# Attention and FFN in one kernel: weight loads after the first U transpose, a 64-row FFN tile of two chunks computed as a pair, and new planner constants

## The chip, the cores and the metric

One core of a Trainium2 chip. The metric is the device time of one execution in microseconds; the profile's span runs from the first to the last profiled instruction of that core.

## The reference

S = 2048 tokens, D = 640, H = 32 query heads of 20 columns, one shared key and value head, FFN width F = 1728, all in bfloat16.

```
xn = layernorm(x)
q = (xn @ wq) in 32 heads of 20;  k = xn @ wk;  v = xn @ wv      # one k and v for all heads
p = softmax(q k^T / sqrt(20));    o = p v                        # per head, 2048 x 2048
h = silu(xn @ w1)                                                # 1728 columns
return x + concat(o) @ wo + h @ w2
```

## The kernel before, in words

**Order.** The kernel holds its own planner. Every operation is an `Op` with an engine, a planned duration and dependencies; `Sched` lets engines and planned times run, picks for each engine the next operation that is ready, and writes down one fixed order per engine. The waits are semaphores between these orders. So a changed constant or a changed operation can move instructions anywhere on any engine. SP issues nearly all DMAs, in its order.

**Attention.** The queries are cut into four chunks of 512 (`QC = 4`). A unit is one head of one chunk, 128 in all; three units make a group, and the 43rd group has two. A group has 16 steps, one for each block of 128 keys (688 steps in all). In a step:

- `do_S` issues the score matmuls, one for each unit, in tiles of 32 rows of the PE array side by side (L773), into three PSUM banks; steps use two sets of banks in turn.
- ACT takes the exponential of two or three of the units in one instruction (L791, 1024 or 1536 columns).
- In most steps `want_dve` gives the third unit to DVE instead, which forms the exponential from integer bits: L805 clips the scores into `Z`, L873 adds a constant for up to three such blocks at a time, and POOL adds another one (L811). The three versions are added up with different weights in the PV matmuls.
- `pv_mm` issues the value matmuls (L861), four tiles of 32 columns side by side, into one bank (`UBANK`). Those that use POOL's sum (the "thirds") are put together by `flush_z`.

`want_dve` refuses steps named in `KT_ACT`, the first eight steps, and steps at which the work planned for DVE exceeds `DVE_TH`.

**End of a group.** `end_group` copies the bank to `U` on DVE (L976). `norm_dma` transposes `U` into `UT` by a DMA from SP (L935), POOL reads the result (L946, L943, L948), DVE takes reciprocals (L953) and POOL writes the normalized heads into `o` (L962). For the very last group PE does the transpose (L988).

**Jobs between the steps.** `step` fills PE's time between score matmuls with PV passes or with the next matmul of a job, taken in order from one queue: query projections (`qd_job`, L1054, evicted on DVE and spread to `qT` by some seven DMAs from SP, L1070), FFN first layer (`h_job`, L1090; tanh on ACT, L1098, and a product on DVE, L1103, since silu is made from tanh), and output jobs (`out_job`, FFN second layer L1152, attention output L1157). `fill_chunk` lists the jobs of a chunk and their earliest steps; `H_FIRST` FFN jobs come before the output jobs of the chunk before. `fill` adds matmuls on zeros where PE would be idle (L697, L710). When few slots of the exponentials' ring are left (`PV_PRESS`), PV goes first.

F = 1728 makes 13 tiles of 128 rows and one of 64 (`FLAST`); each of the four chunks computes all 14 (`fk` 0 to 13), five matmuls each. The second layer uses the 64-row tile with `w2[0:64, 13]`.

**Late loads.** `late_loads` issues from SP what is needed later: 14 pieces of `w2` (L1336), five of `wo` (L1519), and a fill of the second half of `qT` from `tb` (L1512, 1 MB). POOL then scales `wo` in place (L1522, five times). It is called with a key on which the loads depend: in `qd_job`, at the first query job of chunk 0. `tb[0]` is also where the tanh of even FFN tiles goes.

**End of the kernel.** Behind the last step stand the last output jobs: first `hold_job` (L1215, L1220), which opens banks with the residual and the attention output of four blocks, then the last block of heads, transposed on PE (L1130, evicted at L1135), and the closing matmuls (L1157), ACT and DVE evictions (L1184, L1187) and output DMAs (L1191).

Of the kernel before, what the change touches and what calls it, by code (L numbers as in the profile page):

```python
# [14 lines left out]
P = 128  # L15
# [3 lines left out]
DC = 5  # L19
SLOT = 32  # L20
BANK = 512
QW = 512
# [5 lines left out]
FC = 14  # L28
FLAST = F - 13 * P
# [16 lines left out]
NBLK = 31  # L46
NZ = 4
ZB = 3
AHEAD = 30
Q_FROM = 8  # L50
H0_STEP = 10
KT_ACT = ()
Y_POOL = True
Y_TIME = 0.72
Y_LOCK = False
Y_SLOW = 0.1
H_FIRST = 8
NEARLY = 2
LASTPV = 16
DVE_LAST = 1  # L60
ZWAIT = 6
SWITCH = 0.105
S_LEAD = 0.56
PV_PRESS = 8
DVE_TH = 2.6
U_PRIO = 1.1
X_PRIO = 0.8
PACE = (0.9, 0.9, 0.9, 0.9)
# [273 lines left out]


class Job:
    def __init__(self, name, mms, reads, consume, gate=None, min_step=-1, banks=None, on_start=None, width=0, hold=None, use=None):
# [10 lines left out]
        self.use = use  # L356


class Builder:
# [371 lines left out]
    def do_mm(self, job, now, d):  # L731
        work, fn = job.mms.pop(0)
        job.begun = True
        b = job.bank
        op = self.sc.new("pe", d, lambda pe: fn(pe, b), job.reads, [("B", b)], name=job.name, queue=False)
        op.work = min(work, 0.009) if job.name[0] == "v" else min(work, 0.053) if job.name[0] == "t" else work
# [17 lines left out]
    def do_S(self, t, now):  # L754
        sc = self.sc
        g, kt = divmod(t, KT)
# [10 lines left out]
        def fn(pe):  # L767
            ins = None
            for j, x in enumerate(us):
# [7 lines left out]
        op = sc.new("pe", 0.216 + self.switch("S"), fn, self.s_reads(t, dv), [("B", par3 + j) for j in range(nh)],  # L777
                    name=f"S{t}", queue=False)
# [36 lines left out]
        first = kt == 0  # L815
        last = kt == KT - 1

        if dv:
            y = self.Y[:, zs, 0, zp * QW:(zp + 1) * QW].bitcast(BF16)
            z = self.Z[:, zs, zp * QW:(zp + 1) * QW].bitcast(BF16)  # L820
        thirds = []

        def pfn(pe):
# [9 lines left out]
            for x in thirds:  # L833
# [3 lines left out]
                    name=f"PV{t}", mode="PV", queue=False)  # L837
# [10 lines left out]
        if self.zblocks and (len(self.zblocks) >= (ZB if g < self.NG - 2 else 2) or t - self.zblocks[0][0] >= ZWAIT  # L848
                             or t == self.T - 1 or (kt == KT - 1 and g >= FLUSH_G)):
            self.flush_z()  # L850
        self.move_pv()
        if last:
            self.end_group(g)
# [10 lines left out]
    def flush_z(self):  # L864
        sc = self.sc
        zs = self.zset
        n = len(self.zblocks)
        self.zset = (self.zset + 1) % NZ
        zk = [("Z", zs, i) for i in range(n)]
        Z = self.Z[:, zs, 0:n * QW]  # L870
        w = n * QW
        for k in range(1 if self.y_on_pool else 2):
            sc.new("dve", Y_SLOW + t_dve_4x(w), lambda v, k=k: v.tensor_scalar(  # L873
                self.Y[:, zs, k, 0:n * QW], Z, float(PH[k + 1][0]), None, ALU.add), zk,
                [("Y", zs, k, i) for i in range(n)], prio=4.0 + 0.1 * k, name=f"y{k}").lock = True
        ts = []
        for i, (t, pv) in enumerate(self.zblocks):
            ks = [("Z", zs, i), ("Y", zs, 0, i)]
            pv.deps |= sc.deps_of(ks, ())
            for k in ks:  # L880
                sc.readers[k].append(pv)
            x = self.Y[:, zs, 1, i * QW:(i + 1) * QW].bitcast(BF16)
            kt = t % KT

            def th(pe, q, x=x, kt=kt):
                if q >= 2:
                    return self.pv_mm(pe, q, 2, kt, x, False, False)
# [3 lines left out]
        first = self.zblocks[0][1]  # L891
        end = self.pv_wait[-1][0].kt == KT - 1
        tail = self.pv_wait.pop() if end else None
        seen = False
        for op, _ in self.pv_wait:
            seen = seen or op is first
            if seen and self.can_host(op) and ts:
                self.host(op, ts.pop())
        if end and self.can_host(tail[0]) and len(self.thirds + ts) % 3 == 1:
            self.host(tail[0], ts.pop() if ts else self.thirds.pop())  # L900
        self.thirds += ts
        while len(self.thirds) >= 3 or (end and self.thirds):
            part = self.thirds[:3]
# [12 lines left out]
            self.pv_wait.append((op, False))  # L916
        if tail is not None:
            self.pv_wait.append(tail)
        self.zblocks = []

    def can_host(self, op):
        return op.after is not None and not op.after and op.kt < KT
# [8 lines left out]
    def norm_dma(self, g, rows):  # L931
        sc = self.sc
# [4 lines left out]
        op.dur = UT_ISSUE  # L937
        self.ut_cnt[up] += 1
        op.inc_no = self.ut_cnt[up]
        ut = self.UT[:, up, :, :].rearrange("p q (i j) -> p q i j", j=SLOT)  # L940
        w = self.W
        if rows == P:
# [104 lines left out]
    def qd_job(self, c, m, step=-1):  # L1047
# [10 lines left out]
        def consume(b):  # L1058
            sl = self.nqd % 2
            self.nqd += 1  # L1060
            sc.new("dve", t_dve_ps(QW), lambda v: v.tensor_scalar(self.qd[0:rows, sl, :], self.bk(b, 0, QW, 0, rows), C1,
                                                                  None, ALU.mult), [("B", b)], [("qd", sl)],
                   prio=X_PRIO, name=f"qev{c}_{m}")
            sem = sc.sem(f"q{c}_{m}")
            ops = []
            heads = range(lo // DH, -(-hi // DH))
            for h in heads:
                a, z = max(lo, h * DH), min(hi, h * DH + DH)
                r = (h % 4) * SLOT + a - h * DH
                ops.append(sc.dma("sp", lambda q, a=a, z=z, r=r, h=h: q.dma_start(  # L1070
                    self.qT[r:r + z - a, h // 4, c % 2, :], self.qd[a - lo:z - lo, sl, :]), [("qd", sl)],
                    [("qb", c % 2, h)], (z - a) * QW * 2, sem=sem, name="qdma"))
                ops[-1].dur = 0.74
            sc.note(ops[-1], (), [("q", c, h, lo) for h in heads])
            for op in ops:
                op.inc_no = len(ops)
            if c == 0 and m == 0:
                self.late_loads(("qd", sl))
        reads = [("xnT", 4 * c + i) for i in range(4)] + [("wqd", 0), ("wqd", 1)]
        if c >= 2:  # L1080
            step = max(step, self.first_step[c - 1] + KT)
# [1 line left out]

    def h_job(self, c, fk, step):
        sc = self.sc
        rows = P if fk < FC - 1 else FLAST
        mms = []
        for k in range(DC):
            def f(pe, b, k=k):
                return pe.matmul(self.bk(b, 0, QW, 0, rows), self.w1[:, k, fk * P:fk * P + rows],  # L1090
                                 self.xnT[:, k, c * QW:(c + 1) * QW], start=(k == 0), stop=(k == DC - 1))
            mms.append((t_mm(QW), f))

        def consume(b):
# [6 lines left out]
            if c == 0:  # L1101
# [4 lines left out]
        reads = [("xnT", 4 * c + i) for i in range(4)] + [("w1",)]  # L1106
        return Job(f"h{c}_{fk}", mms, reads, consume, min_step=step, width=QW if rows == P else 0)

    def try_oT(self, c):
        last = c == QC - 1  # L1110
# [29 lines left out]
    def out_job(self, c, i, e, step=-1, ffn=True, ks=range(DC), src="xres", dst="ost", hmax=H):  # L1140
# [5 lines left out]
        tot = (FC if ffn else 0) + len(ks)  # L1146
        if ffn:
            for fk in range(FC):
                rows = P if fk < FC - 1 else FLAST

                def f(pe, b, fk=fk, rows=rows, m=len(mms)):
                    return pe.matmul(self.bk(b, 0, 320), self.hT[0:rows, fk, i * P:(i + 1) * P],  # L1152
                                     self.w2[0:rows, fk, e0:e0 + 320], start=(m == 0), stop=(m == tot - 1))
                mms.append((t_mm(320), f))
        for k in ks:
            def f(pe, b, k=k, m=len(mms)):
# [76 lines left out]
    def fill_chunk(self, c, t):  # L1233
# [58 lines left out]
    def prologue(self):  # L1292
# [370 lines left out]
```

## Time and profile before

| what | us |
|---|---|
| median of 6 runs | 738.34 |
| lowest, highest run | 736.34, 739.56 |
| the profiled execution, time | 736.35 |
| the profiled execution, span | 734.6 |
| first score matmul of the last group (L773) | 706.45 |
| last score matmul (L773) | 719.16 |
| U copied for the first transpose, DVE L976 | 50.50 to 51.19 |
| first U transpose, SP L935: issued, landed | 55.10, 61.13 |
| qT fill behind the late loads, SP L1512: issued, landed | 54.36, 60.56 |

Group rows read: line, engine, operation, out<-in with shapes, count, then busy time and the mean of one in ns, then idle time of the engine just before and what ended it. Window rows read: stretch, then busy time and count on PE, PE's weight loads, DVE, ACT and POOL, then granted PE clock, share of the DMA engines, GB/s. Wait rows: who waited for whom, total, times, longest. Timeline rows: start, length, engine, line, with the idle time before in brackets. Busy time is the union of instructions that can overlap: consecutive ones on an engine can start less than a duration apart.

### The profile page before, as it was taken

How to read it: one execution, taken by the hardware profiler on the slowest of the kernel's cores; microseconds unless marked ns; L12 is line 12 of the kernel's file. 1: busy time of each engine (PE TensorE's matmuls, PEld its weight loads, DVE VectorE, ACT ScalarE, POOL GpSimd, SP SyncE). 2: the span in 40 equal slices, each digit the busy share in tenths (PEclk: the TensorE clock that was granted, in tenths of full speed). 3: DMA queues.
4: the chain of work that ended last, by engine and by line, in shares of the span. 5: the costliest groups of instructions: out<-in, count | busy, mean ns of one | idle time of the engine just before them, and what ended most of it. 6: DMA issues, size and time to landing. Idle time of an engine off the chain costs nothing.

```text
span 734.6 us, 18666 instructions
## 1 busy us (share of the span) xinstructions
PE 704.0 (96%) x6746; PEld 228.8 (31%) x6798; DVE 650.7 (89%) x1180; ACT 701.8 (96%) x782; POOL 516.0 (70%) x886
## 2 busy tenths in 40 slices
PE   9897999999999999999999999999999999999997
PEld 4421222233332232223332223323333222233334
DVE  7776999989999899999899899999889889899895
ACT  6997999999999999999999999999999999999972
POOL 4366777767787777677778667767687767777763
PEclk9999999999999999999999999999999999999999
DMA  9573000000002011100001112100003001100021
GB/s 280 122 231 94 16 21 16 22 17 16 9 17 44 8 53 40 42 16 2 16 8 31 23 26 57 48 18 8 10 8 45 16 9 49 40 9 8 9 44 37
DMA packets 58465, 29.12 MB, mean 40 GB/s; under 512 B 44390, under 2 KB 57734, under 8 KB 58374
## 3 DMA queue, kind: packets, MB, share of 16 engines
q1 hardware_dynamic: 56918, 27.71, 14.9%
q8 instruction: 55, 0.90, 0.5%
q10 hardware_dynamic: 1456, 0.22, 0.2%
q14 instruction: 36, 0.29, 0.1%
HBM read 11.36 MB, written 2.62 MB: 19 GB/s over the span
## 4 chain that ended last, share of the span: by engine, by line
PE 69%; ACT 15%; DVE 9%; issue 5%; POOL 1%; DMA 1%; DVEq 0%; ACTq 0%; POOLq 0%
PE psall L861 23%; PE psall L773 22%; ACT sbt L791 12%; PE psall L1152 9%; PE psall L1090 7%; DVE sbt L805 5%; PE psall L1054 2%; PE psall L1157 2%; PE psall L710 2%; DVE sbt L873 1%; ACT sbt L1098 1%; DVE sbt L976 1%; PE psall L697 1%; ACT sbt L1441 1%; DMA sbt<-sbt 1%
## 5 line engine op out<-in xcount | busy, mean ns | idle before, releaser
L791 ACT ACTIVATE sbt<-psall 128x1024 bf16<-128x1024 f32 (+2 forms) x688 | 667.2, 1103 | 13.0 <-PE psall L773 11.2
L811 POOL TENSOR_TENSOR sbt<-sbt 128x256 int32<-128x256 int32 x626 | 429.1, 693 | 169.3 <-DVE sbt L805 120.7
L805 DVE TENSOR_SCALAR sbt<-psall 128x512 int16<-128x512 f32 x626 | 418.4, 683 | 46.0 <-PE psall L773 38.3
L773 PE MATMUL psall<-sbt 32*128 32x512 bf16 x2048 | 269.4, 384 | 12.9 <-ACT sbt L791 6.2
L861 PE MATMUL psall<-sbt 128*32 128x512 bf16 x3470 | 262.8, 384 | 3.5 <-POOL sbt L811 2.8
L773 PEld LDWEIGHTS psall<-sbt 32*128 32x128 bf16 x2048 | 69.3, 91 | 251.3 <-ACT sbt L791 85.9
L873 DVE TENSOR_SCALAR sbt<-sbt 128x1536 int16<-128x1536 int16 (+1 forms) x218 | 131.5, 604 | 3.2
L861 PEld LDWEIGHTS psall<-sbt 128*32 128x32 bf16 x3470 | 66.0, 94 | 111.3 <-issue 70.7
L1152 PE MATMUL psall<-sbt 128*128 128x320 bf16 x448 | 87.7, 303 | 0.0
L1090 PE MATMUL psall<-sbt 128*128 128x512 bf16 (+1 forms) x245 | 76.0, 384 | 4.5 <-issue 2.9
L1152 PEld LDWEIGHTS psall<-sbt 128*128 128x128 bf16 x448 | 33.4, 97 | 44.8 <-issue 35.1
L1103 DVE SCALAR_TENSOR_TENSOR sbt<-sbt,psall 128x512 bf16<-128x512 bf16 (+1 forms) x56 | 38.1, 680 | 8.5 <-PE psall L773 4.4
L1098 ACT ACTIVATE sbt<-psall 128x512 bf16<-128x512 f32 (+1 forms) x56 | 37.9, 678 | 0.0
L1090 PEld LDWEIGHTS psall<-sbt 128*128 128x128 bf16 (+1 forms) x280 | 19.3, 98 | 41.3 <-issue 25.9
L976 DVE CAST sbt<-psall 128x512 bf16<-128x512 f32 x43 | 29.3, 681 | 1.8 <-PE psall L861 1.6
L1157 PE MATMUL psall<-sbt 128*128 128x320 bf16 x144 | 27.8, 302 | 1.1 <-DVE sbt L1135 0.7
L962 POOL TENSOR_TENSOR sbt<-sbt 128x240 bf16<-128x240 f32 (+2 forms) x44 | 25.7, 584 | 3.7 <-DVE sbt L953 3.1
L1054 PE MATMUL psall<-sbt 128*128 128x512 bf16 (+1 forms) x81 | 25.4, 384 | 1.8 <-issue 1.3
L948 POOL TENSOR_TENSOR sbt<-sbt 128x44 f32<-128x44 f32 x84 | 25.1, 299 | 1.1
L946 POOL CAST sbt<-sbt 128x168 f32<-128x168 bf16 x42 | 14.1, 335 | 15.2 <-DMA sbt<-sbt 15.0
L710 PE MATMUL psall<-sbt 128*128 128x512 bf16 (+3 forms) x71 | 18.7, 415 | 2.2 <-POOL sbt L1351 1.5
L1157 PEld LDWEIGHTS psall<-sbt 128*128 128x128 bf16 x144 | 11.5, 97 | 15.2 <-issue 10.6
(86 smaller groups left out, 206.5 us busy)
## 6 DMA issues: line engine op xcount, KB each, us to landing
sbt<-in_A_x_dram SPq DMA_DIRECT2D x32, 160.0 KB, 3.3
out_dram<-sbt SPq DMA_DIRECT2D x15, 160.0 KB, 1.9
sbt<-in_B_w_dram SPq DMA_DIRECT2D x5, 432.0 KB, 6.2
sbt<-sbt SPq DMA_DIRECT2D x105, 20.0 KB
sbt<-in_B_w_dram SPq DMA_DIRECT2D x13, 160.0 KB, 3.6
sbt<-sbt SPq DMA_TRANSPOSE x68, 2.5
sbt<-sbt SPq DMA_DIRECT2D x1, 1024.0 KB, 6.2
sbt<-in_A_wo_dram SPq DMA_DIRECT2D x5, 160.0 KB, 3.0
```

Of the source, the lines that this page charges most:

```text
L773: ins = pe.matmul(self.bk(par3 + j), self.kT[r:r + SLOT, kk, kt * P:(kt + 1) * P], self.qT[r:r + SLOT, h // 4, (x // H) % 2, :], start=Tru ...
L791: return a.activation(self.E[:, b0 * QW:(b0 + na) * QW], self.ps[:, par3 * BANK:(par3 + na) * BANK], AF.Exp, scale=ACT_SCALE)
L805: return v.tensor_scalar(self.Z[:, zs, zp * QW:(zp + 1) * QW], self.bk(bb), 0.0, ZMAX, ALU.max, ALU.min)
L811: sc.new("pool", Y_TIME, lambda v: v.tensor_tensor(self.Y[:, zs, 1, zp * QW:(zp + 1) * QW].bitcast(I32), self.Z[:, zs, zp * QW:(zp + 1) * ...
L861: return pe.matmul(self.bk(UBANK, 0, QW, q * SLOT, (q + 1) * SLOT), self.v[:, w, kt, :], x, start=start, stop=stop, tile_position=(0, q * ...
L873: sc.new("dve", Y_SLOW + t_dve_4x(w), lambda v, k=k: v.tensor_scalar(self.Y[:, zs, k, 0:n * QW], Z, float(PH[k + 1][0]), None, ALU.add), z ...
L1054: return pe.matmul(self.bk(b, 0, QW, 0, rows), self.wq[:, k, lo:hi], self.xnT[:, k, c * QW:(c + 1) * QW], start=(k == 0), stop=(k == DC - 1))
L1090: return pe.matmul(self.bk(b, 0, QW, 0, rows), self.w1[:, k, fk * P:fk * P + rows], self.xnT[:, k, c * QW:(c + 1) * QW], start=(k == 0), s ...
L1098: sc.new("act", t_act(QW), lambda a: a.activation(t, src, AF.Tanh, scale=0.5), [("B", b)], [("tb", tp)], prio=X_PRIO, name=f"th{c}_{fk}")
L1103: sc.new("dve", t_dve_ps(QW), lambda v: v.scalar_tensor_tensor(out=self.hT[0:rows, fk, :], in0=t, scalar=1.0, in1=src, op0=ALU.add, op1=AL ...
L1152: return pe.matmul(self.bk(b, 0, 320), self.hT[0:rows, fk, i * P:(i + 1) * P], self.w2[0:rows, fk, e0:e0 + 320], start=(m == 0), stop=(m = ...
L1157: return pe.matmul(self.bk(b, 0, 320), self.oT[:, k, i * P:(i + 1) * P], self.wo[:, k, e0:e0 + 320], start=(m == 0 and src != "ps"), stop= ...
```

## The change

1. The late loads hang on the copy of `U` in `norm_dma` of group `LATE_G = 0`, and are recorded behind its transpose, no longer in the first query job.
2. The 64-row FFN tile is computed only by even chunks, for their own chunk and the next: for each of the five blocks two matmuls in two column tiles of 64 columns, chunk c into rows 0 to 63 of the bank and chunk c + 1 into rows 64 to 127; one tanh and one product for both. The odd chunk reads rows 64 to 127 of `hT` and of `w2`, whose last 64 rows are loaded a second time.
3. Constants: `KT_ACT` (0,) in place of (), so the first step of a group gives nothing to DVE; `DVE_TH` 3.4 for 2.6; `PV_PRESS` 12 for 8; `H_FIRST` 4 for 8.
4. Thirds left over at the end of a group are emitted also when no block waits (`emit_thirds`, the second half of `flush_z`, now a function of its own).

In the instruction order that the planner makes of it, L805 (L808 in the new file) occurs 637 times instead of 626, POOL's addition as often; L861's matmuls 3534 times instead of 3470.

```diff
+LATE_G = 0
-KT_ACT = ()
+KT_ACT = (0,)
-H_FIRST = 8
+H_FIRST = 4
-PV_PRESS = 8
-DVE_TH = 2.6
+PV_PRESS = 12
+DVE_TH = 3.4
...
             self.flush_z()
+        elif last and self.thirds:
+            self.emit_thirds([], None)
...
         op.inc_no = self.ut_cnt[up]
+        if g == LATE_G:
+            self.late_loads(("U", up))
...
-            if c == 0 and m == 0:
-                self.late_loads(("qd", sl))
...
     def h_job(self, c, fk, step):
-        rows = P if fk < FC - 1 else FLAST
+        rows = P
+        pair = fk == FC - 1
...
-                return pe.matmul(self.bk(b, 0, QW, 0, rows), self.w1[:, k, fk * P:fk * P + rows],
-                                 self.xnT[:, k, c * QW:(c + 1) * QW], start=(k == 0), stop=(k == DC - 1))
+                if not pair:
+                    return pe.matmul(self.bk(b), self.w1[:, k, fk * P:(fk + 1) * P], self.xnT[:, k, c * QW:(c + 1) * QW],
+                                     start=(k == 0), stop=(k == DC - 1))
+                for z in range(2):
+                    ins = pe.matmul(self.bk(b, 0, QW, z * FLAST, (z + 1) * FLAST), self.w1[:, k, fk * P:fk * P + FLAST],
+                                    self.xnT[:, k, (c + z) * QW:(c + z + 1) * QW], start=(k == 0), stop=(k == DC - 1),
+                                    tile_position=(0, z * FLAST), skip_group_check=True)
+                return ins
...
-                rows = P if fk < FC - 1 else FLAST
+                r0 = FLAST * (c % 2) if fk == FC - 1 else 0
+                r1 = r0 + FLAST if fk == FC - 1 else P
...
-                    return pe.matmul(self.bk(b, 0, 320), self.hT[0:rows, fk, i * P:(i + 1) * P],
-                                     self.w2[0:rows, fk, e0:e0 + 320], start=(m == 0), stop=(m == tot - 1))
+                    return pe.matmul(self.bk(b, 0, 320), self.hT[r0:r1, fk, i * P:(i + 1) * P],
+                                     self.w2[r0:r1, fk, e0:e0 + 320], start=(m == 0), stop=(m == tot - 1))
...
-        hs = [(3.0, lambda s, fk=fk: self.h_job(c, fk, s)) for fk in range(FC)]
+        hs = [(3.0, lambda s, fk=fk: self.h_job(c, fk, s)) for fk in range(FC) if fk < FC - 1 or c % 2 == 0]
...
-            w2p.append(lambda q, fk=fk, rows=rows: q.dma_start(self.w2[0:rows, fk, :],
-                                                               self.B_w2[fk * P:fk * P + rows, :]))
+            for r0 in ((0,) if rows == P else (0, FLAST)):
+                w2p.append(lambda q, fk=fk, rows=rows, r0=r0: q.dma_start(self.w2[r0:r0 + rows, fk, :],
+                                                                          self.B_w2[fk * P:fk * P + rows, :]))
```

More of the change, by code (lines that the diff above doesn't have):

```diff
@@ L344, with __init__ @@
 class Job:
-    def __init__(self, name, mms, reads, consume, gate=None, min_step=-1, banks=None, on_start=None, width=0, hold=None, use=None):
+    def __init__(self, name, mms, reads, consume, gate=None, min_step=-1, banks=None, on_start=None, width=0, hold=None, use=None, n=1):
         self.name = name
@@ L356, in __init__ @@
         self.use = use
+        self.n = n
 class Builder:
@@ L735, in do_mm @@
         op = self.sc.new("pe", d, lambda pe: fn(pe, b), job.reads, [("B", b)], name=job.name, queue=False)
+        op.mm = job.n
         op.work = min(work, 0.009) if job.name[0] == "v" else min(work, 0.053) if job.name[0] == "t" else work
@@ L890, in flush_z, with emit_thirds @@
             ts.append((th, ("Y", zs, 1, i), kt))
-        first = self.zblocks[0][1]
+        self.emit_thirds(ts, self.zblocks[0][1])
+        self.zblocks = []
+    def emit_thirds(self, ts, first):
+        sc = self.sc
         end = self.pv_wait[-1][0].kt == KT - 1
@@ L918, in flush_z @@
             self.pv_wait.append(tail)
-        self.zblocks = []
     def can_host(self, op):
@@ L1105, in consume @@
                 [("B", b), ("tb", tp)], ks, prio=X_PRIO, name=f"hp{c}_{fk}")
-        reads = [("xnT", 4 * c + i) for i in range(4)] + [("w1",)]
-        return Job(f"h{c}_{fk}", mms, reads, consume, min_step=step, width=QW if rows == P else 0)
+        reads = [("xnT", 4 * c + i) for i in range(8 if pair else 4)] + [("w1",)]
+        return Job(f"h{c}_{fk}", mms, reads, consume, min_step=step, width=0 if pair else QW, n=2 if pair else 1)
     def try_oT(self, c):
@@ L1148, in out_job, with f @@
             for fk in range(FC):
-                rows = P if fk < FC - 1 else FLAST
-                def f(pe, b, fk=fk, rows=rows, m=len(mms)):
-                    return pe.matmul(self.bk(b, 0, 320), self.hT[0:rows, fk, i * P:(i + 1) * P],
-                                     self.w2[0:rows, fk, e0:e0 + 320], start=(m == 0), stop=(m == tot - 1))
+                r0 = FLAST * (c % 2) if fk == FC - 1 else 0
+                r1 = r0 + FLAST if fk == FC - 1 else P
+                def f(pe, b, fk=fk, r0=r0, r1=r1, m=len(mms)):
+                    return pe.matmul(self.bk(b, 0, 320), self.hT[r0:r1, fk, i * P:(i + 1) * P],
+                                     self.w2[r0:r1, fk, e0:e0 + 320], start=(m == 0), stop=(m == tot - 1))
                 mms.append((t_mm(320), f))
```

## The prediction

> **What bounds the kernel now.** I read the busy table first, then the groups by shape, the windows by stage, the waits of the worst window, the timeline there, and the end.
>
> ```profile
> span 734.6 us, 18666 instructions
> ...
> PE 704.0 (96%) x6746; PEld 228.8 (31%) x6798; DVE 650.7 (89%) x1180; ACT 701.8 (96%) x782; POOL 516.0 (70%) x886
> ```
> ```profile
> L791 ACT ACTIVATE sbt<-psall 128x1024 bf16<-128x1024 f32 x614 | 584.3, 1075 | 10.5 <-PE psall L773 9.2 <-PE psall L861 0.5
> L1098 ACT ACTIVATE sbt<-psall 128x512 bf16<-128x512 f32 x52 | 35.6, 684 | 0.0
> ```
> ```profile
> 60.00:80.00 20.00, 15.14 (x133) 4.31 (x131) 13.36 (x23) 15.30 (x17) 17.59 (x32) 0.91 0.05 11
> 80.00:700.00 620.00, 605.07 (x5879) 188.81 (x5926) 565.20 (x968) 617.56 (x674) 452.78 (x763) 1.00 0.10 23
> ...
> 719.00:735.00 16.00, 11.44 (x98) 6.76 (x96) 7.49 (x19) 2.64 (x6) 2.73 (x5) 0.95 0.12 41
> ```
> PE and ACT are level in the first table (the columns of the windows are PE, weight loads, DVE, ACT, POOL, clock, DMA), so the stage decides. Between 80 and 700 us ACT is busy 617.56 of 620: the exponentials (L791) and the FFN's tanh (L1098) set the pace. These durations overlap: from one start to the next the trace has 905 ns for a 128x1024 row, 1331 for 128x1536, 478 for tanh. Laid out over the 16 steps of a head group, these spacings give the measured length of groups 3 to 40 within about a microsecond (group 10: 14.90 against 14.92; group 6: 16.33 against 16.71). From the last score matmul (719.16 us) on, ACT is nearly idle and PE runs to the end. One window stands out, 60 to 80 us:
>
> ```profile
> POOL sbt L946 <- DMA sbt<-sbt: 5.2, 1, 5.2
> ACT sbt L791 <- PE psall L773: 4.7, 3, 2.9
> DVE sbt L953 <- POOL sbt L948: 4.0, 1, 4.0
> ```
> ```profile
> 54.36 0.69 SPq L1512 DMA_DIRECT2D sbt<-sbt  x1
> 55.10 16.95 SPq L935 DMA_TRANSPOSE sbt<-sbt  x2
> ```
> The first U transpose (L935) is issued at 55.10, right behind the last late load (the 1 MB fill L1512, landing at 60.56), and lands after 6.0 us; the other transposes have a median of 2.4. POOL (L946) waits 5.2 us for it, DVE's reciprocal (L953) 4.0 for POOL, PE for POOL's L811, ACT 4.7 for PE.
>
> **The change part by part.** I count from the order of instructions of the two programs, which has no times.
>
> *A, late loads.* They move from behind the first query job to behind the first U transpose: 15 w2 pieces, 5 of wo, the fill. U's eviction ended at 51.19, so the transpose can now be issued near 51.3 and land by 53.7, before POOL asks (55.99). The stall cost ACT the 4.7 us of that row plus some 0.17 (1075 less 905 ns) hidden in each of its three instructions: 5.2. But 21 DMAs now stand before the second U transpose. SP from 52.5: 15 x 0.47 + 5 x 0.49 + 0.69, free at 62.7. The first lands 2.3 us after its issue (54.8), and landings followed each other by about 0.55 us before: 54.8 + 19 x 0.55 = 65.2, the fill 3.0 more, 68.2, the transpose 0.6 behind it (as 61.13 after 60.56), 68.8. Its eviction stands behind the 25th L805 on DVE (about 62 us), and POOL asks after 29 of its additions, near 66.4: it waits 2.4 us, with wo's five scalings (5 x 0.72) behind it. Before, PE ran on from 55.99 to 60.47 while POOL stood still, so a cover of some 4.5 us exists; if it is used up, all 2.4 reach ACT. I take 1.0: gain 4.2, ends 0 (the stall comes back whole) and 5.2. The first tanh needs the fill landed (it overwrites tb); it stands behind the 47th exponential now, near 72 us.
>
> [...] In this trace PE was idle 2.76 us from 60.47, then 0.64, and these windows followed (the clock is the last column but two):
> ```profile
> 63.00:64.00 1.00, 0.48 (x5) 0.12 (x5) 0.56 (x2) 0.00 (x0) 1.00 (x4) 1.00 0.00 0
> ...
> 66.00:67.00 1.00, 1.00 (x6) 0.11 (x3) 0.00 (x0) 0.00 (x0) 1.00 (x3) 0.50 0.00 0
> ```
> [...]
>
> *B, less work on ACT.* L805 goes from 626 to 637: eleven more 512-column blocks on DVE, each turning a 1331 ns exponential into one of 905: 11 x 0.426 = 4.7. Half-width FFN tiles go from four jobs to two: 2 x 0.478 = 0.96. Sum 5.65, all between 43 and 706 us, where ACT is the bound. Ends: 0 (PE takes over) and 5.65. DVE pays 11 x 0.609 - 2 x 0.605 = 5.5 us and POOL 11 x 0.69 = 7.6; with 72 us and 218 us idle they have room, DVE needing about 14.6 of the 16 us of a full group. Uncovered it would be those 5.5 us.
>
> *C, the block near the end.* At 698.25 PE ran eight FFN and six PV passes between two score steps, and ACT waited:
> ```profile
> 701.45 1.02 ACT L791 ACTIVATE sbt<-psall 128x1024 bf16<-128x1024 f32 x1 [1.85 <-PE psall L773]
> ```
> In the new order no such stretch of that group holds more than five PV passes (1.48 us). Gain 1.7 (ends 0 and 1.85). Elsewhere, stretches of over 1.35 us fall from 51 to 37; I price that at nothing.
>
> *D, PE.* In passes (matmuls in different tiles side by side count once): PV 889 to 901 (+12 x 0.216 = 2.6), half-width FFN 20 to 10 (-2.2), fills -0.9, and 1452 changes between score, PV and full matmuls become 1472 (+20 x 0.098; a change costs 314 ns against 216) = 2.0. Together +1.5, beside ACT up to the last score step: 0. Its end without that cover is +1.5, in the second rival.
>
> *E, the end.* Here the change loses. Before, 34 passes of 320 columns from the output and FFN jobs stand behind the last score step, now 90: chunk 3's FFN jobs have slipped back, since fewer microseconds of ACT leave PE fewer in which to place them, and the first tanh moves back eleven steps. 56 x 0.136 = 7.6 us of PE work with no ACT work beside it. Before, PE stood still 0.69 us for the transposed last block; now the passes fill that, and three of them lie between PV passes that wait for DVE (0.4). I take +6.5; ends 5.7 (all idle of PE there filled) and 7.6.
>
> ```profile
> 725.39 1.26 PE L1157 MATMUL psall<-sbt 128*128 128x320 bf16 x8 [0.69 <-DVE sbt L1135]
> ```
>
> *F, small.* The last w2 tile is loaded twice, 64 rows each: one more issue, 0.47 us on SP, already in A's sum. [...]
>
> Sum: -4.2 - 5.65 - 1.7 + 0 + 6.5 = -5.05 us. The profiled execution took 736.35 around its span of 734.6 and becomes 731.3, its span 729.6. It lies 2.0 below the median of 738.34, so the median becomes 733.3.
>
> **The rivals.**
> - *The stall moves along.* The second U transpose meets the loads as the first did: A is 0, the sum -0.85, the median 737.5. For it: POOL's wait (2.4) plus the scalings (3.6) exceed the 4.5 us of cover. Against: 2.4 us are half of the 5.2 of before, and on their own within the cover. 12%.
> - *Slower: PE takes over as the bound.* Its 605.07 of 620 us and 69% of the chain speak for it. Then B and C do not reach the end and D's +1.5 does: -4.2 + 1.5 + 6.5 = +3.8, median 742.1. With D's 1.5 on the path, it makes the kernel slower by over 1.5 us once less than 2.3 of the 7.35 us of B and C comes through. Against: by passes and changes a group takes PE 14.3 to 16.1 us, below ACT's 14.9 to 16.8 in most groups, and ACT idles 0.4% from 80 to 700. 10%.
> - *The pair does not run side by side.* Then D has ten passes more, 10 x 0.216 = 2.2 us; if all of it shows, -2.9 and 735.4. Against: L861's tiles of 32 columns start 3 ns apart. 6%.
>
> **How the numbers follow.** The forecast has 72%, and its time is 733.3 us. With the ends of its terms it reaches from -7.0 (731.3) to about -2 (736.3); the range from 730.0 to 737.6 adds the first rival and the third, and leaves the slower one out. About 0.2% (1.5 us) is what a measurement of this kernel tells from no change. Faster by more: most of the forecast, nearly all of the third rival and a third of the first, 0.79. Slower by more: the second rival and a little of the first, 0.11. Within: 0.10.
>
> **What would show it.** A: a first U transpose landing in about 2.4 us, POOL's L946 (L956 then) waiting 2 to 3 us at the second near 66 us, ACT idle below 1.5 us from 60 to 80, the clock at 1.00. B: 637 rows of L808, ACT still above 99% from 80 to 690. E: last score step near 707.5 us, and some 22 us from there to the end against 15.4. It would be wrong if ACT idles by more than 1% in the long stage, if the second transpose costs ACT over 3 us, or if the end takes less than 20 us.

## The result, and the profile after

The changed kernel takes 733.53 us (median of 20 runs, 733.06 to 736.66); the kernel before, measured beside it, takes 737.09 (46 runs). The ratio is 0.9956, 95% interval 0.9947 to 0.9966: 3.2 us faster (2.5 to 3.9; the two medians alone differ by 3.6). The prediction had 733.3 us. That it is so close is partly luck: the kernel before came out 1.25 us below the 738.34 that the prediction started from, and this hides most of a gain that was smaller than expected, 3.2 us where it had 5.05.

The first lines of the page of the changed kernel, and its shares of the chain that ended last:

```profile
span 732.8 us, 18837 instructions
...
PE 706.1 (96%) x6814; PEld 229.6 (31%) x6863; DVE 653.1 (89%) x1189; ACT 695.9 (95%) x780; POOL 525.0 (72%) x897
...
PE 65%; ACT 22%; issue 6%; DVE 4%; DMA 1%; POOL 1%; ACTq 0%; DVEq 0%; POOLq 0%
```

ACT has 5.9 us less to do than before, its share of the chain grew (15% to 22%), and the span fell by only 1.8 us. The profiled execution took 734.58, a microsecond above its median, and that of before was a little below its own, so the ratio is the measure of the gain and the traces tell where it lies. For that I cut each trace at the starts of the score steps (L773 before, L776 after): step 16 is the start of the second head group, step 64 of the fifth, step 672 of the last (steps counted from 0).

| stretch, us | before | after | difference |
|---|---|---|---|
| steps 16 to 64 (the stretch of the stall) | 53.77 | 49.88 | -3.9 |
| steps 64 to 672 | 609.08 | 602.88 | -6.2 |
| step 672 to the last score step | 12.71 | 12.67 | 0.0 |
| last score step to the end | 15.39 | 23.49 | +8.1 |

Of the 3.9 us in the first row only 2.3 are waiting saved; the rest is work that ACT no longer has in this stretch (two 128x1536 exponentials and two tanh fewer). The last score step starts at 709.28 us instead of 719.16, 9.9 us earlier, and four fifths of that are lost behind it. The windows by stage show the same (columns: PE, weight loads, DVE, ACT, POOL, granted clock, DMA share, GB/s):

```profile
60.00:80.00 20.00, 17.50 (x155) 4.94 (x153) 15.26 (x25) 17.68 (x19) 15.37 (x25) 0.91 0.42 124
...
80.00:700.00 620.00, 605.12 (x5956) 186.76 (x5999) 571.59 (x985) 617.59 (x680) 466.24 (x785) 1.00 0.10 24
...
719.00:735.00 16.00, 10.37 (x73) 6.67 (x70) 4.63 (x10) 1.53 (x4) 0.00 (x0) 0.97 0.12 42
```

Between 60 and 80 us ACT was busy 15.30 us before and 17.68 now. Up to 700 us it is still the busy engine; in the last 16 us it has 1.53 us of work.

**The stall.** SP's own queue, with the time of issue and how long the issues took:

```profile
50.67 1.23 SPq L943 DMA_TRANSPOSE sbt<-sbt  x1
52.23 7.36 SPq L1353 DMA_DIRECT2D sbt<-in_B_w_dram  x15
59.64 3.32 SPq L1536 DMA_DIRECT2D sbt<-in_A_wo_dram  x5
63.00 0.70 SPq L1529 DMA_DIRECT2D sbt<-sbt  x1
63.75 22.39 SPq L943 DMA_TRANSPOSE sbt<-sbt  x2
```

The first U transpose goes out at 50.67 and lands at 53.69. The 15 w2 pieces, wo and the fill follow; the second transpose, issued at 63.75, lands at 69.44, 0.8 us after the fill (68.65). What waited from 60 to 80 us:

```profile
POOL sbt L956 <- DMA sbt<-sbt: 2.5, 1, 2.5
...
ACT sbt L794 <- PE psall L776: 2.3, 3, 1.3
```

POOL's wait is half of the 5.2 of before and sits at the second transpose, as forecast. What follows it was not in the sum, only in the prediction's reading of the clock row. PE stands still once for long, 1.56 us, and the clock falls:

```profile
73.40 0.40 PE L866 MATMUL psall<-sbt 128*32 128x512 bf16 x4 [1.56 <-POOL sbt L814]
```
```profile
74.00:76.00 2.00, 2.00 (x20) 0.51 (x17) 1.89 (x4) 1.69 (x3) 2.00 (x4) 0.76 0.04 8
76.00:78.00 2.00, 2.00 (x14) 0.39 (x6) 1.27 (x2) 1.63 (x2) 2.00 (x4) 0.50 0.00 0
78.00:80.00 2.00, 1.67 (x11) 0.55 (x11) 0.69 (x1) 1.39 (x2) 2.00 (x4) 0.89 0.00 0
```

**The end.** PE in order of time behind the last score step (start, length, shape, count). Before, its first rows there were:

```profile
719.48 2.12 PE L861 MATMUL psall<-sbt 128*32 128x512 bf16 x28
721.53 1.12 PE L1152 MATMUL psall<-sbt 128*128 128x320 bf16 x7
...
722.61 0.67 PE L1152 MATMUL psall<-sbt 128*128 128x320 bf16 x3
```

and in the changed kernel:

```profile
712.59 1.23 PE L1168 MATMUL psall<-sbt 128*128 128x320 bf16 x7
...
713.88 2.17 PE L1168 MATMUL psall<-sbt 128*128 128x320 bf16 x14
...
716.22 6.39 PE L1168 MATMUL psall<-sbt 128*128 128x320 bf16 x42
722.54 2.35 PE L1173 MATMUL psall<-sbt 128*128 128x320 bf16 x16
```

L1168 is the second FFN matmul. PE runs it without a gap for 6.39 us in one row, with nothing for ACT or DVE to do but evictions: this is the work that had been placed among the score steps before.

**The pair.** Its row of the groups:

```profile
L1103 PE MATMUL psall<-sbt 128*64 128x512 bf16 x20 | 3.1, 391 | 0.0
```

Twenty half-width matmuls took PE 6.2 us before (L1090, the same 391 ns each); two at a time, they take 3.1.

### The profile page after: what moved, and what is told of

Same layout as the page of the kernel before. It is cut to its first block, busy times and chain, and to the rows that moved or that the text cites. A ratio compares the mean times of both kernels' runs of the same rounds, so it can differ in the third digit from the quotient of the medians.

```text
span 732.8 us, 18837 instructions
## 1 busy us (share of the span) xinstructions
PE 706.1 (96%) x6814; PEld 229.6 (31%) x6863; DVE 653.1 (89%) x1189; ACT 695.9 (95%) x780; POOL 525.0 (72%) x897
## 3 DMA queue, kind: packets, MB, share of 16 engines
q1 hardware_dynamic: 56998, 27.79, 14.9%
## 4 chain that ended last, share of the span: by engine, by line
PE 65%; ACT 22%; issue 6%; DVE 4%; DMA 1%; POOL 1%; ACTq 0%; DVEq 0%; POOLq 0%
PE psall L866 22%; PE psall L776 21%; ACT sbt L794 20%; PE psall L1168 8%; PE psall L1100 7%; PE psall L1064 2%; PE psall L1173 2%; PE psall L712 2%; ACT sbt L1113 1%; DVE sbt L808 1%; DMA sbt<-sbt 1%; PE psall L699 1%; ACT sbt L1458 1%; DVE sbt L1438 0%; DVE sbt L1118 0%
## 5 line engine op out<-in xcount | busy, mean ns | idle before, releaser
L814 POOL TENSOR_TENSOR sbt<-sbt 128x256 int32<-128x256 int32 x637 | 437.3, 692 | 160.6 <-DVE sbt L808 144.3
L808 DVE TENSOR_SCALAR sbt<-psall 128x512 int16<-128x512 f32 x637 | 425.1, 683 | 48.4 <-PE psall L776 43.3
L776 PE MATMUL psall<-sbt 32*128 32x512 bf16 x2048 | 269.4, 384 | 12.2 <-ACT sbt L794 8.7
L866 PE MATMUL psall<-sbt 128*32 128x512 bf16 x3534 | 269.2, 385 | 2.1 <-POOL sbt L814 1.6
L776 PEld LDWEIGHTS psall<-sbt 32*128 32x128 bf16 x2048 | 69.3, 91 | 245.7 <-ACT sbt L794 79.3
L1168 PE MATMUL psall<-sbt 128*128 128x320 bf16 x448 | 85.4, 302 | 0.2 <-DVE sbt L1118 0.2
L1100 PE MATMUL psall<-sbt 128*128 128x512 bf16 x228 | 70.8, 384 | 4.0 <-issue 3.2
L1168 PEld LDWEIGHTS psall<-sbt 128*128 128x128 bf16 x448 | 34.7, 97 | 43.7 <-issue 32.7
L1118 DVE SCALAR_TENSOR_TENSOR sbt<-sbt,psall 128x512 bf16<-128x512 bf16 x54 | 36.8, 681 | 2.5 <-ACT sbt L1113 0.7
L1113 ACT ACTIVATE sbt<-psall 128x512 bf16<-128x512 f32 x54 | 37.1, 687 | 0.0
L1100 PEld LDWEIGHTS psall<-sbt 128*128 128x128 bf16 x260 | 17.8, 97 | 40.9 <-issue 26.6
L1064 PE MATMUL psall<-sbt 128*128 128x512 bf16 (+1 forms) x81 | 25.1, 384 | 1.0 <-issue 0.6
L712 PE MATMUL psall<-sbt 128*128 128x512 bf16 (+1 forms) x68 | 18.0, 422 | 2.1 <-POOL sbt L1368 1.5
L1185 DVE SCALAR_TENSOR_TENSOR sbt<-psall,sbt 128x320 bf16<-128x320 f32 x28 | 13.6, 484 | 6.1 <-PE psall L1168 5.9
```

Of the source, the lines that this page charges most:

```text
L776: ins = pe.matmul(self.bk(par3 + j), self.kT[r:r + SLOT, kk, kt * P:(kt + 1) * P], self.qT[r:r + SLOT, h // 4, (x // H) % 2, :], start=Tru ...
L808: return v.tensor_scalar(self.Z[:, zs, zp * QW:(zp + 1) * QW], self.bk(bb), 0.0, ZMAX, ALU.max, ALU.min)
L814: sc.new("pool", Y_TIME, lambda v: v.tensor_tensor(self.Y[:, zs, 1, zp * QW:(zp + 1) * QW].bitcast(I32), self.Z[:, zs, zp * QW:(zp + 1) * ...
L866: return pe.matmul(self.bk(UBANK, 0, QW, q * SLOT, (q + 1) * SLOT), self.v[:, w, kt, :], x, start=start, stop=stop, tile_position=(0, q * ...
L1064: return pe.matmul(self.bk(b, 0, QW, 0, rows), self.wq[:, k, lo:hi], self.xnT[:, k, c * QW:(c + 1) * QW], start=(k == 0), stop=(k == DC - 1))
L1100: return pe.matmul(self.bk(b), self.w1[:, k, fk * P:(fk + 1) * P], self.xnT[:, k, c * QW:(c + 1) * QW], start=(k == 0), stop=(k == DC - 1))
```

## The experiments

Twelve kernels, each timed beside the kernel before on the same chip. Stretches are in us as above; in e5, e6, e7, e9 and e10 the two score matmuls of step 672 start 0.2 us apart, and the later one is taken. "Lost" is the time from one start of ACT to the next beyond the spacings of the prediction (905, 1331 and 478 ns), summed from step 16 to 64 and from 64 to 672; "behind" is the time from the last score step to the end, and the number of FFN and output passes of 320 columns there; "tanh" the score step of the first and of the last tanh, counted from 1.

| kernel | ratio (95%) | 16 to 64 | 64 to 672 | behind | lost | tanh |
|---|---|---|---|---|---|---|
| before | 1 | 53.77 | 609.08 | 15.39, 34 | 5.8, 14.9 | 37, 622 |
| the change | 0.9956 (0.9947 to 0.9966) | 49.88 | 602.88 | 23.49, 90 | 3.5, 12.8 | 48, 651 |
| e1 | 1.0084 (1.0068 to 1.0100) | 51.67 | 611.38 | 23.09, 90 | 4.6, 16.4 | 47, 656 |
| e2 | 1.0052 (1.0038 to 1.0066) | 56.75 | 604.03 | 23.50, 90 | 10.1, 14.2 | 38, 651 |
| e3 | 1.0045 (1.0032 to 1.0058) | 52.09 | 603.69 | 24.05, 87 | 4.8, 13.5 | 37, 654 |
| e4 | 1.0046 (1.0032 to 1.0060) | 56.77 | 611.62 | 14.18, 20 | 9.7, 18.2 | 38, 618 |
| e5 | 0.9867 (0.9849 to 0.9885) | 48.70 | 602.19 | 18.89, 57 | 1.0, 14.0 | 25, 635 |
| e6 | 0.9865 (0.9844 to 0.9886) | 48.71 | 601.77 | 18.70, 57 | 1.1, 13.6 | 25, 635 |
| e7 | 0.9863 (0.9845 to 0.9880) | 48.68 | 602.16 | 18.93, 57 | 1.0, 14.0 | 25, 635 |
| e8 | 0.9907 (0.9890 to 0.9924) | 50.26 | 608.93 | 13.10, 20 | 1.4, 17.8 | 22, 612 |
| e9 | 0.9915 (0.9895 to 0.9934) | 51.17 | 606.70 | 11.48, 8 | 3.0, 19.1 | 21, 618 |
| e10 | 0.9937 (0.9918 to 0.9956) | 51.27 | 608.63 | 11.47, 8 | 3.3, 20.0 | 21, 622 |
| e11 | 0.9968 (0.9958 to 0.9979) | 51.80 | 608.70 | 16.04, 34 | 3.0, 15.2 | 22, 622 |
| e12 | 0.9925 (0.9907 to 0.9942) | 48.53 | 606.91 | 18.00, 47 | 1.2, 27.2 | 24, 640 |

### One part at a time

**e1, the loads alone.** The kernel before, with

```
+        if g == LATE_G:
+            self.late_loads(("U", up))
...
-            if c == 0 and m == 0:
-                self.late_loads(("qd", sl))
```

> The kernel before with the late loads alone moved behind the first U transpose; constants and FFN tiles as before. Theory (the steady stage is set by ACT, and PE work that finds no place there is paid behind the last score step): the stall of 60 to 80 us shrinks by 3.5 to 4.5 us, but the first tanh waits for the qT fill and the FFN jobs slip: 90 passes of 320 columns behind the last score step in place of 34, +8 us. Together 2 to 5 us slower than before, about 740 against 737. Rival (the loads are the whole gain of the change): 3 to 4 us faster, about 733.5.

742.89 us, 6 us slower and beyond the 2 to 5 expected. The stall shrinks by less than expected (lost 5.8 to 4.6), 90 passes stand behind the last score step in place of 34, which costs 7.7 us there, and the steps from 64 to 672 take 2.3 us more. Moved alone, the loads do harm. The last column names a candidate: with the 1 MB fill late, the first tanh moves from step 37 to 47, because it writes tb, from which the fill reads.

**e2, all but the loads.** The changed kernel, with the loads back behind the first query job (the diff of e1 the other way round).

> The changed kernel with the late loads back at the first query job. Theory: the stall of 60 to 80 us comes back (ACT idle there 4 to 5 us), 90 passes stand behind the last score step as in the changed kernel, so 3 to 5 us slower than the changed kernel, level with the kernel before (736.5 to 738.5). Rival (DVE's eleven blocks are the whole gain and the stall is made up elsewhere): as fast as the changed kernel, 733.5.

740.68 us: slower by more than expected. The stall is larger than it was before the change:

```profile
POOL sbt L954 <- DMA sbt<-sbt: 9.2, 2, 8.7
ACT sbt L794 <- PE psall L776: 9.1, 2, 7.9
```
```profile
60.00:62.00 2.00, 0.00 (x0) 0.00 (x0) 0.00 (x0) 0.00 (x0) 0.00 (x0) 0.50 1.10 241
...
66.00:68.00 2.00, 2.00 (x16) 0.46 (x14) 0.44 (x2) 1.85 (x2) 2.00 (x4) 0.50 0.03 8
```

POOL asks earlier here, near 54.1 us (62.78 less 8.7) against 55.99, and the transpose, issued at 56.77, lands at 62.78 instead of 61.13. POOL waits 8.7 us in place of 5.2; PE stands still, and after it has work again it runs on at a clock of 0.50. Beside the other parts of the change, moving the loads is worth 0.96% (1.0052 against 0.9956), 7 us, not 4.2.

**e3, the constants alone.** The kernel before, with

```
-KT_ACT = ()
+KT_ACT = (0,)
-H_FIRST = 8
+H_FIRST = 4
-PV_PRESS = 8
-DVE_TH = 2.6
+PV_PRESS = 12
+DVE_TH = 3.4
...
+        elif last and self.thirds:
+            self.emit_thirds([], None)
```

> The kernel before with the four constants of the change (and the thirds left over at a group's end emitted), loads and FFN tiles as before. Theory: ACT loses 4.7 us and the long block before the last group 1.7, but 87 passes in place of 34 stand behind the last score step, +7.8: 0 to 2.5 us slower than before, about 738. Rival (ACT's saved time reaches the end): 4 to 6 us faster, about 732.

740.06 us, 3.3 us slower, beyond the 0 to 2.5 expected. The score steps from 64 to 672 take 5.4 us less and the end takes 8.7 us more, with 87 passes behind; step 16 also starts 1.4 us later than before.

**e4, the pair alone.** The kernel before, with the pair's lines of the diff (the two column tiles, the second load of the last w2 tile, one job for two chunks). This kernel, e8 and e11 also keep the change's fourth item, the thirds left over at a group's end.

> The kernel before with the pair of 64-row FFN tiles alone. Theory: ten PE passes (2.16 us) and two tanh (0.96) go; behind the last score step 20 passes in place of 34 (-2.0 us): 2 to 4 us faster than before, about 734. Rival (the pair is hidden beside ACT but for the tanh): 0.5 to 1.2 us faster.

740.04 us: a miss, 3 to 4 us slower where 2 to 4 faster was expected. The end does shorten, by 1.2 us. What was not seen is that the pair's extra load stands ahead of the first U transpose here, which is issued at 56.42 (before 55.10) and lands at 62.83:

```profile
POOL sbt L954 <- DMA sbt<-sbt: 6.9, 1, 6.9
```
```profile
66.00:68.00 2.00, 1.46 (x11) 0.31 (x15) 1.21 (x2) 1.02 (x1) 2.00 (x4) 0.50 0.00 0
...
72.00:74.00 2.00, 2.00 (x10) 0.43 (x11) 1.74 (x3) 1.52 (x3) 2.00 (x6) 0.50 0.00 0
```

The wait is 6.9 us instead of 5.2, the clock is at 0.50 from 66 to 74 us, and ACT loses 9.7 us where it lost 5.8. Whether that comes from the extra load alone or from the changed order around it, this run does not separate. The stretch of the stall takes 3.0 us more, and the steps from 64 to 672 take 2.5 us more as well, with ACT losing 18.2 us there where it lost 14.9; for that no cause is shown.

So each part alone makes the kernel slower: e1, e3 and e4 add up to +12.9 us (0.84 + 0.45 + 0.46% of 737), while all three together give -3.2. They cannot be priced one by one against the kernel before.

### What makes the end long

**e5, another source for the fill.** The changed kernel, with

```
-        tb = self.tb[:, 0, :]
+        tb = self.ost[:, 0, 0:QW]
...
-            rep = bass.AP(self.tb, tb.offset, ...)
+            rep = bass.AP(self.ost, tb.offset, ...)
```

and the same for the instruction that writes the source and for the names of what is read and written.

> The changed kernel, but the 1 MB fill of the score operands is read from the output staging buffer instead of from tb, so that the first tanh (which writes tb) need not stand behind the fill's landing. In the order of instructions the first tanh comes earlier, more FFN jobs fit ahead of the last score step, and 57 passes of 320 columns are left behind it instead of 90. Theory 'the late tanh makes the end long': 33 passes x 0.147 us = 4.9 us less behind the last score step, last score step still near 709.3, ratio to the kernel before about 0.989 (728.6 against 736.8). Rival 'PE's total is what is conserved': the passes move ahead of the last score step and push it back by as much, ratio 0.994 to 0.997, last score step near 712 to 714.

727.91 us, a little faster than the first theory's 728.6: the end gives 4.6 us, and the last score step is 2.9 us earlier too (706.36), which neither theory had. The first tanh runs at step 25 instead of 48, the last at 635 instead of 651. The passes left behind are 33 fewer (139 ns each), and the steps before did not get longer: 602.19 against 602.88. The window of the stall is clean too:

```profile
60.00:80.00 20.00, 19.54 (x184) 5.88 (x183) 18.22 (x30) 19.67 (x23) 16.58 (x28) 1.00 0.39 120
```

ACT 19.67 of 20 us, clock 1.00: in this order POOL waits 0.7 us for the second transpose, not 2.5. The end, on PE:

```profile
710.20 1.23 PE L1168 MATMUL psall<-sbt 64*128 64x320 bf16 x7
...
712.89 2.17 PE L1168 MATMUL psall<-sbt 128*128 128x320 bf16 x14
715.00 2.35 PE L1173 MATMUL psall<-sbt 128*128 128x320 bf16 x16
```

The row of 42 passes is gone; the rest is as in the changed kernel.

**e6 and e7, the fill in other places.** e6 leaves it behind the first query job, e7 puts it behind the second U transpose (and reads it from ost):

```
+            if c == 0 and m == 0:
+                self.late_fill(("qd", sl))
```
```
+        if g == LATE_G + 1:
+            self.late_fill(("U", up))
```

> The changed kernel with the 1 MB fill back behind the first query job, and only the w2 and wo loads behind the first U transpose. 57 passes behind the last score step. The second U transpose should find SP and the queue free near 63, so POOL's wait of 2.47 us there falls to under 0.5 us and ACT's 2.3 us with it; if the fill delays the first U transpose, 16 to 64 grows by up to 3 us again. Theory 'the stall is all the gain and the tail can be had too': 726 to 729 us. Rival 'PE's total is conserved': 731 to 734.

> The changed kernel with w2 and wo behind the first U transpose, and the fill behind the second, read from the output staging buffer. 57 passes behind the last score step. Neither U transpose stands behind the fill: the second should land within 3 us of its issue, ACT's wait in 60 to 80 us should fall from 2.3 to under 1 us and the clock there to 0.95 or more. Theory: 16 to 64 some 1 to 2 us shorter than 49.88, end 4.9 us shorter: 726 to 729 us. Rival 'PE's total is conserved': the end's part comes back ahead of the last score step, 731 to 733.

727.72 and 727.23 us. The three agree within their intervals and, but for 0.4 us from 64 to 672, within 0.2 us in every stretch, although the fill is issued at three different places. What they share is a first tanh at step 25. So the place of the fill hardly matters; that the first tanh need not wait for it does.

The step of the first tanh does not fix the number of passes by itself. With the new constants it is 57 passes at step 25, but 90 both at 38 (e2) and at 48 (the change). With the old ones it is 90 at step 47 (e1), and 34 both at 37 (before) and at 22 (e11, below).

### What each part is worth without the late tanh

**e11, the loads alone, once more.** The kernel before, with the w2 and wo loads behind the first U transpose, and the fill left where it was.

> The kernel before with only the w2 and wo loads moved behind the first U transpose; the 1 MB fill stays behind the first query job, so that the first tanh need not wait. 34 passes behind the last score step as before, 625 blocks (before 626). Theory 'the stall is worth what it cost, and e1 lost only by the late tanh': steps 16 to 64 in 50 to 50.5 us against 53.8, the rest as before, 3 to 4 us faster than before (733 to 734). Rival 'the stall moves along': POOL waits over 2 us at the second U transpose and the time is within 1.5 us of before.

734.61 us, 0.32% (2.4 us) faster than before: between the two theories. 34 passes behind as before, and the last tanh at step 622 as before: e1's long end came with the late fill. But the stretch of the stall still takes 51.80 us, since a part of the wait remains:

```profile
PEld psall L866 <- DVE sbt L878: 1.9, 2, 1.6
POOL sbt L956 <- DMA sbt<-sbt: 1.8, 1, 1.8
```

**e8, loads and pair, without the constants.** e6 with the four constants of the kernel before.

> e6 with the four constants of the kernel before (the moved w2 and wo loads and the pair, without the eleven blocks that DVE takes from ACT). 20 passes behind the last score step. Theory 'the constants only move time from the score steps to the end': steps 64 to 672 near 609 us (against 603 with the new constants), end near 14.2 us, total within 2 us of e6. Rival 'the constants pay by themselves': e6 faster than this one by 3 to 6 us.

730.37 us. The first theory's parts hold roughly (608.93 for 609, 13.10 for 14.2), but e8 is 2.65 us above e6 where it had at most 2: the constants gain 7.2 us from 64 to 672 and 1.6 ahead of it, and give 5.6 back behind the last score step. 0.9907 against 0.9865 of e6, intervals apart: they pay 0.42%, 3 us. That is the lower edge of the other theory.

**e9, fewer passes behind.** e7 with one constant back:

```
-PV_PRESS = 12
+PV_PRESS = 8
```

> e7 with one constant back at its old value, PV_PRESS 8 in place of 12: in the order of instructions DVE keeps its 637 blocks, the passes of 320 columns behind the last score step fall from 57 to 8, and PE changes between score, PV and full matmuls 14 times less. Theory 'the long end comes from the order in which the planner places the FFN, not from a lack of PE time': PE was busy 614.4 of the 620 us from 80 to 700 in e7, so 5.6 us are free there, and 49 passes x 0.147 = 7.2 us less 14 x 0.098 = 1.4 us of changes just fit: the end falls by 7 us (18.96 to about 12), the last score step moves by 0 to 3 us, 720 to 723 us. Rival 'PE is the bound by now': what leaves the end comes back ahead of the last score step, 725.5 to 727 us.

731.10 us, 3.9 us slower than e7: both missed. The first theory had a gain of 4 us or more. The rival was right that what leaves the end comes back ahead of it, but it had 725.5 to 727 us and no loss. The end takes 7.4 us less, and the stretches before it 9.7 more (2.5 + 4.5 + 2.6 from step 672 to the last). ACT's waits from 64 to 700 us in e7, then in e9:

```profile
ACT sbt L794 <- PE psall L776: 3.1, 7, 0.9
```
```profile
ACT sbt L794 <- PE psall L776: 7.3, 7, 2.2
```

The passes come back as a few long waits of ACT for a score matmul. And the end itself becomes thinner than its chain of waits:

```profile
723.68 0.45 PE L1233 MATMUL psall<-sbt 128*128 128x320 bf16 x2 [0.52 <-DVE sbt L1152]
```

PE's busy time cannot decide this: the two traces hold 6016 and 5946 matmul records from 80 to 700 us, and some are missing (e7 has 260 matmuls of 128x512 in the first FFN layer, L1102, and e9 only 229 for the same 260 weight loads). The 5.6 free microseconds that I counted on came from such a sum.

**e10, e9 without the pair.** The pair's lines of the diff taken out of e9; 637 blocks and 8 passes behind in both.

> e9 without the pair (four half-width tiles with a tanh each, in place of two pairs); 637 blocks and 8 passes behind the last score step as in e9, so that the two differ by the pair alone. The prediction's prices: 2 x 0.478 = 0.96 us of ACT, or 10 x 0.216 = 2.2 us of PE where PE sets the pace. Theory 'ACT is the bound': e10 slower than e9 by about 1 us. Rival 'PE is the bound': by about 2 us. If the pair is worth nothing: the same within 0.5 us.

732.31 us, 1.2 us above e9 (0.9937 against 0.9915; the intervals overlap). The size is that of the two tanh saved on ACT, 0.96 us; the difference by itself is not certain.

**e12, more blocks on DVE.** e9 with

```
-KT_ACT = (0,)
+KT_ACT = ()
-DVE_TH = 3.4
+DVE_TH = 3.0
```

> e9 with KT_ACT empty and DVE_TH 3.0: 660 blocks on DVE in place of 637, 923 PV passes in place of 901, 16 changes less, 47 passes behind the last score step in place of 8. Theory 'ACT is still the bound': 23 x 0.426 = 9.8 us less up to the last score step, 39 x 0.147 = 5.7 us more behind it, 4 us faster than e9. Rival 'PE is the bound by now', the prediction's slower case: 22 x 0.216 = 4.8 us of PV more, 1.6 of changes less, 3 us slower than e9.

731.34 us, the same as e9: both theories missed, in opposite directions. Of the 23 blocks that leave ACT, 21 do so from step 64 to 672, which is 8.9 us by their price, and that stretch gets no shorter (606.91): what ACT loses there rises by 8.1 us, from 19.1 to 27.2. Its waits from 64 to 700 us:

```profile
ACT sbt L794 <- PE psall L776: 11.6, 24, 2.3
```

The end takes 6.5 us more, and what pays for that is the first stretch (48.53 against 51.17), the last group (2.7 us less) and the time ahead of step 16. By here ACT is no longer the bound of the long stretch.

## Why the prediction was right, and where it was not

The side of the result and the time were right; the gain was 3.2 us of 5.05, and three steps were off.

*A, late loads: right in mechanism, mis-sized.* First transpose landed at 53.69 (53.7 forecast, with some luck: it was issued 0.6 us earlier than forecast and took 3.0 us instead of 2.4), second at 69.44 (68.8), POOL waits 2.47 (2.4). Forecast was that 1.0 of it reaches ACT. In the stretch ACT loses 3.5 us instead of 5.8, so A was worth 2.3 against the kernel before, not 4.2 (taken out of the whole change, it is worth 7: e2). The step that failed is the choice of 1.0, and with it the clock: that the wait left over costs no clock was my estimate, and the changed kernel goes against it, since 1.56 us of standing still were followed by a window at 0.50. The trace of before had the same behind a gap of 2.76 us: the window from 66 to 67 us at 0.50, with ACT waiting all through it (1.50 us, up to 67.48). With those 1.50 us left standing, A would have been 2.7, the better number. Two of the signs did not come: ACT idles 2.3 us from 60 to 80 (below 1.5 forecast), and the clock there is 0.91, not 1.00. A condition that I wrote for being wrong, "the second transpose costs ACT over 3 us", was nearly met: three waits of 2.3 us in sum, and 2.7 us in starts that came late by over 0.3.

*B, less on ACT: right.* 637 blocks on DVE and 54 tanh, as counted. Of the 9.9 us up to the last score step, A has 2.3 and C 1.4; the remaining 6.2 stand against 5.65. The trace has the forecast work gone, eleven 128x1536 exponentials and two tanh; the rest lies in smaller waits, since ACT's lost time from 64 to 672 fell by 2.1 us, 0.7 more than C. ACT was busy 617.59 of 620 us from 80 to 700. One number was off without effect: DVE's idle time, given as 72 us, is 83.9 over the span (734.6 less 650.7).

*C: right.* The start that came 1.97 us late before, at 701.45, is gone, the largest left there is 0.54: 1.4 us against 1.7.

*D: right for this kernel.* PE's additions did not show up to the last score step. The pair ran side by side: 20 matmuls of 391 ns each in 3.1 us, against 6.2 before.

*E, the end: right in sign, low by 1.6 us.* 90 passes as counted, 8.1 us against 6.5 for 56 more. A pass of the FFN's output averaged 150 ns in the row of 42 (716.22 to 722.54), not the 136 of a pass of the same tile, since each job changes once to a tile of 64 rows, and that start comes 232 ns after the one before, the next one 238 ns after it. Behind the PV passes the end grew by 7.2 us: 53 passes more at 0.150, less the 0.69 of idle that they fill, are 7.3. The three others of the 56 lie between PV passes, and the 0.4 us that were to be hidden there were not: from the last score step to the end of its PV passes it takes 3.31 us against 2.37 before. Of the two reasons given for the 90, neither stands as given. The eleven steps by which the first tanh moves back are not needed for it: e2 has it at 38 and still 90 (though with the old constants they suffice by themselves: e1). What does help, and is shown, is to have it earlier than in the kernel before: e5, at 25, has 33 of the 56 gone. The other reason, fewer microseconds of ACT, is only half shown: e3 has 87 with the constants alone, but e9 moves 49 passes with one constant of the order and the same 637 blocks. The prediction noted that the first tanh would stand behind the fill, and priced this only as passes at the end; it did not see that this wait could be taken out.

*F, small.* The 15 pieces took 7.36 us on SP and the second transpose was 0.6 us later than forecast; whether the second load of 64 rows has a part in that, these runs do not separate.

*The rivals.* "The stall moves along" held in part: the wait went to the second transpose and took 1.9 of the 4.2 us. "The pair not side by side" fell. "PE takes over" fell for this kernel, as 64 to 672 is 6.2 us shorter; but it begins a short way on: in e9 and e12 the work that leaves ACT or the end comes back as ACT's waits for PE.

The expected gain went three ways, then: 1.9 us stayed in the stall, 0.3 in C and 1.6 in the longer end, while B with the smaller waits was 0.5 better; that leaves the 1.8 us of the profiled pair. The timed runs have 3.2; single executions scatter (step 16 alone starts anywhere from 42.3 to 45.3 us in these kernels), so the terms are good to about a microsecond.

The best version is e7, with e5 and e6 the same within their intervals: 0.9863 of the time before, 1.4% faster, where the change itself has 0.4%.

## What to carry to other kernels

When a load is moved to a later place, look at who writes the buffer that it reads or reads the one it fills: a fill that ties up a scratch buffer delayed the first tanh by 23 steps, and the FFN behind it was still 16 steps late 600 us later. Where one engine sets the pace and another is nearly as full, time saved on the first can be paid back as work left over for the second at the end (here 8.1 of 9.9 us), so price the end with every change of order. Parts of a change can each be a loss alone and a gain together; undo one part at a time from the whole as well as adding one to the old kernel.

## What the hardware showed that was not expected

The clock of PE fell to 0.50 after 1.56 us without work in the changed kernel (the window from 76 to 78 us). The length of one stop does not decide it: in e9 a stop of 1.72 us was followed by no fall.

```profile
78.85 1.05 PE L866 MATMUL psall<-sbt 128*32 128x512 bf16 x16 [1.72 <-POOL sbt L814]
```
```profile
78.00:80.00 2.00, 1.15 (x19) 0.43 (x19) 2.00 (x4) 0.52 (x1) 2.00 (x3) 1.00 0.12 31
80.00:82.00 2.00, 1.84 (x13) 0.52 (x11) 1.69 (x3) 1.73 (x2) 2.00 (x4) 1.00 0.05 12
```

What does decide it, these runs do not show. In e2 the clock fell within a stop of 7.8 us (57.1 to 64.9), was still at 0.50 from 66 to 68 us, with PE at work again, and back at 1.00 from 70. A DMA transpose between on-chip buffers lands 2.4 us after its issue in the median (the 42 of L935 before, and the 42 of L943 in the changed kernel; in e5, one issued at 68.12 landed at 70.54), 3.0 us after in the first of the changed kernel (50.67 to 53.69), and 5.7 to 6.4 us after where it is issued right behind the 1 MB fill (the change: 63.75 to 69.44; e4: 56.42 to 62.83). After a change from tiles of 128 rows to one of 64, a pass starts 232 ns after the one before, where passes of the same tile follow at 136 (320 columns, L1168 of the changed kernel).
